# One row of wq ahead of K, and V in one load: reordering the head of a load stream in a decode kernel

## The chip, the cores and the metric

The kernel runs on one core of one Trainium2 chip. The metric is the device time of one execution in microseconds (us), as the median of several runs. The engines are named as in the profile: PE (TensorE) for matrix products, PEld for its weight loads, DVE (VectorE), ACT (ScalarE), POOL (GpSimd) and SP (SyncE), which here does nothing but issue loads and the store of half the result.

## The reference, cut to what matters

One token `x` of 1,024 elements goes through an attention block A and a channel MLP B side by side, both fed by the same layer norm, and both are added to `x`.

```python
xn = layernorm(x)                                     # 1 x 1024
q  = xn @ wq                                          # wq: 1024 x 4096; 32 heads of 128
k, v = k_cache[:, :, -4096:], v_cache[:, :, -4096:]   # 4 key/value heads, the last 4096 of 65536 positions
o  = softmax(q @ k.T * 128**-0.5) @ v                 # 8 query heads to a key/value head
A  = o @ wo                                           # wo: 4096 x 1024
h  = gelu(layernorm(xn) @ w1 + b1)                    # w1: 1024 x 3584
B  = h @ w2 + b2                                      # w2: 3584 x 1024
return x + A + B
```

All inputs are bfloat16. What has to be read from HBM is wq 8 MB, K 4 MB, V 4 MB, w1 7 MB, w2 7 MB and wo 8 MB, nearly 40 million bytes for a single token; every weight is used once.

## The kernel before, in words

Four large SBUF buffers, `slot[0]` to `slot[3]`, each 128 partitions by 32 KB, are used in turn by all the big tensors. K's four heads lie in `slot[0]`, wq's rows 0 to 3 in `slot[1]`, rows 4 to 7 in `slot[2]`; w1's halves follow in `slot[1]` and `slot[0]`, V in `slot[2]`, w2's rows in `slot[3]` and `slot[1]`, wo in `slot[0]` and `slot[2]`. A "row" of wq here is one of the 8 rows of the matrix that a partition holds: `wq_v = A_wq.rearrange("(p c) n -> p c n", p=128)`, so that `wq_v[:, 0, :]` takes 8 KB to each of 128 partitions, 1 MB in all. A load of several neighbouring rows takes one contiguous piece to a partition: 16 KB for two, 32 KB for four.

The program is recorded as a list (`Plan`): each operation names its engine, the keys that it reads and those that it writes. `Plan.emit` turns that into one instruction stream to an engine, in the order of the list, with the semaphore waits that the keys demand. There is no scheduler that reorders. All big loads go through SP's queue in the order of the list; an SP load waits until the readers of its buffer's last contents are done, and what is behind it on SP waits too.

Only the loads of K (`load_k`, four, one to a head, 32 partitions of 32 KB each, L192) and of `x32` (on ACT, L197) stand ahead of the list: they are issued at once, before a barrier that all engines pass at the program's beginning. SP then issues wq in three loads (`wq_cuts`, rows 0 and 1, rows 2 and 3, rows 4 to 7), the two biases, and later w1, V, w2 and wo (all at L211, the helper `dma`).

The steps that the text refers to, in their order:

- POOL makes small constant matrices, PE and DVE make the layer norm (L273 to L311); DVE then turns K in 32 x 32 blocks into `slot[3]` (L332, four transposes, each waits for all four K loads), and DVE (L341) and ACT (L337) copy the blocks into `kT`. w1's second half goes into `slot[0]` when K has been transposed, w2's first rows into `slot[3]` when the copies into `kT` are done.
- PE multiplies wq's rows by the normed token as they come: a loop over rows 0 and 1 (L374), two rows written out, a loop over rows 4 to 7 (L383). The sums are cast into `q_sb`, half on DVE (L386) and half on ACT (L387); eight small products and a cast (L415) make `qm`, and 32 products of `qm` with `kT` give the scores (`sc_ps`).
- The softmax follows: maximum, exponential (ACT, L449) and a DVE transpose of the exponentials into `eTb` (L453). w1's products with the second layer norm (`yT`) lie in between, and gelu makes `hT` and `hTf` (L467, L469).
- PE multiplies `eTb` with V in 32 steps, 30 of them in a loop (L494). All 32 wait for `v_in`, the whole of V.
- 21 rows of w2 are summed by DVE (L478, L481), seven by PE; PE multiplies wo's rows (L225), adds DVE's sum (L549 and a product with ones), and two small casts and two stores end the program.

V is loaded in three parts, which PE waits for together:

```python
for g0, g1 in ((0, 2), (2, 3), (3, 4)):
    dma("sp", v4[:, g0:g1, :, :], A_v_cache[0, g0:g1, Sk - W:Sk, :].rearrange("g (p c) d -> p g c d", p=P), (), (f"v{g0}",), ("slot2",))
v_in = ("eTb", "eTb_pad", "v0", "v2", "v3", "slot2")
```

## Time and profile before

| | before |
|---|---|
| median of 3 runs | 101.05 us (100.94 to 101.19) |
| the profiled execution's own time | 100.79 us |
| its span in the profile | 99.0 us |
| bytes moved | 39.88 MB, mean 403 GB/s over the span |
| busy: PE, DVE, ACT, POOL | 59%, 74%, 31%, 10% |
| granted TensorE clock, mean | 0.862 |

The span runs from the first to the last instruction of the profiled execution; some 1.8 us lie around it. The page gives for each engine the busy share, and for 40 equal slices of the span the busy tenths of each engine, the granted TensorE clock and what the 16 DMA engines moved. The chain that ended last is followed back from the last instruction to what released each one. Views by order of time give the start, the duration, the engine, the line, and in brackets the idle time before it with what ended it. Views by stretches give the busy time of each engine, the granted clock, the DMA share and GB/s. The time of a load "to landing" is from its issue on SP's queue.

### The profile page before, as it was taken

How to read it: one execution, taken by the hardware profiler on the slowest of the kernel's cores; microseconds unless marked ns; L12 is line 12 of the kernel's file. 1: busy time of each engine (PE TensorE's matmuls, PEld its weight loads, DVE VectorE, ACT ScalarE, POOL GpSimd, SP SyncE). 2: the span in 40 equal slices, each digit the busy share in tenths (PEclk: the TensorE clock that was granted, in tenths of full speed). 3: DMA queues.
4: the chain of work that ended last, by engine and by line, in shares of the span. 5: the costliest groups of instructions: out<-in, count | busy, mean ns of one | idle time of the engine just before them, and what ended most of it. 6: DMA issues, size and time to landing. Idle time of an engine off the chain costs nothing.

```text
span 99.0 us, 962 instructions
## 1 busy us (share of the span) xinstructions
PE 58.8 (59%) x323; PEld 16.3 (16%) x220; DVE 73.1 (74%) x75; ACT 30.8 (31%) x29; POOL 9.9 (10%) x22
## 2 busy tenths in 40 slices
PE   0032040497300699957995507987671999994791
PEld 0022000122000233402122102212211111110130
DVE  0024699999999999991045956399989999999231
ACT  0230000899998999920020940000000000000001
POOL 0263560000000580000000000000000000000000
PEclk9999999999965557996699985579998557999999
DMA  1999999999999989988999999999897999999970
GB/s 27 397 424 424 424 424 424 424 450 437 437 450 416 488 371 394 533 371 371 430 427 424 430 434 432 442 424 477 371 544 316 437 424 443 430 437 391 409 300 7
DMA packets 3021, 39.88 MB, mean 403 GB/s; under 512 B 454, under 2 KB 460, under 8 KB 844
## 3 DMA queue, kind: packets, MB, share of 16 engines
q1 hardware_dynamic: 2970, 39.86, 94.9%
q8 instruction: 1, 0.02, 0.1%
q10 hardware_dynamic: 50, 0.00, 0.0%
HBM read 39.86 MB, written 0.00 MB: 403 GB/s over the span
## 4 chain that ended last, share of the span: by engine, by line
DMA 64%; PE 23%; issue 3%; SPq 3%; DVE 0%
DMA slot<-in_A_wq_dram 28%; DMA slot<-in_A_wo_dram 21%; DMA slot<-in_A_v_cache_dram 16%; PE qo_ps L494 12%; PE acc L367 10%; SPq L211 3%; PE acc L231 1%; DVE res L568 0%; PE acc L225 0%
## 5 line engine op out<-in xcount | busy, mean ns | idle before, releaser
L337 ACT COPY kT<-slot 32x1024 bf16<-32x1024 bf16 (+1 forms) x18 | 23.9, 1327 | 12.4 <-DVE slot L332 12.2
L481 DVE SCALAR_TENSOR_TENSOR run<-slot,hTf,run 128x1024 f32<-128x1024 bf16 x20 | 24.2, 1271 | 2.5 <-DMA slot<-in_B_w_dram 2.5
L367 PE MATMUL acc<-slot,xw 128*128 x48 | 15.1, 477 | 13.3 <-DMA slot<-in_A_wq_dram 12.7
L332 DVE STREAM_TRANSPOSE slot<-slot 128x4096 bf16<-128x4096 bf16 x4 | 17.4, 4413 | 0.2 <-DMA slot<-in_A_k_cache_dram 0.2
L494 PE MATMUL qo_ps<-slot,eTb 128*128 (+1 forms) x32 | 11.9, 476 | 6.4 <-DMA slot<-in_A_v_cache_dram 4.2
L341 DVE COPY kT<-slot 32x4096 bf16<-32x4096 bf16 x10 | 13.2, 1319 | 0.2
L225 PE MATMUL sc_ps<-slot,o 128*1 128x512 bf16 x48 | 9.1, 379 | 1.6 <-DMA slot<-in_A_wo_dram 1.6
L367 PEld LDWEIGHTS acc<-slot,xw 128*128 x48 | 5.4, 113 | 23.8 <-issue 21.2
L569 ACT CAST res<-acc 33x224 bf16<-33x224 f32 x1 | 0.3, 339 | 20.4 <-PE acc L225 20.4
L225 PE MATMUL sc_ps<-slot,hT 128*1 128x512 bf16 x14 | 6.1, 626 | 0.4 <-DMA slot<-in_B_w_dram 0.4
L494 PEld LDWEIGHTS qo_ps<-slot,eTb 128*128 (+1 forms) x32 | 3.2, 99 | 15.0 <-issue 12.9
L537 ACT CAST o<-misc 128x32 bf16<-128x32 f32 x1 | 0.2, 185 | 17.4 <-PE misc L231 17.4
L225 PE MATMUL sc_ps<-kT,qm 128*32 128x512 bf16 x32 | 5.3, 853 | 0.3 <-DVE qm L415 0.3
L427 DVE COPY sc<-sc_ps 128x512 f32<-128x512 f32 x1 | 0.7, 692 | 4.9 <-PE sc_ps L225 4.9
L217 PEld LDWEIGHTS <-o 128*1 128x1 bf16 x40 | 2.4, 85 | 11.6 <-issue 11.0
L231 PE MATMUL acc<-spread,qm 32*128 32x512 bf16 x4 | 1.6, 498 | 3.7 <-POOL qm L313 3.7
L231 PE MATMUL misc<-x,spread 32*128 32x8 bf16 x4 | 0.3, 168 | 5.8 <-POOL spread L253 5.8
L247 DVE MEMSET mhalf<- 128x1 f32 x1 | 0.1, 59 | 4.6 <-PEq L201 4.6
L225 PE MATMUL acc<-slot,yT 128*1 128x448 bf16 x64 | 3.4, 353 | 0.0
L426 ACT COPY sc<-sc_ps 128x512 f32<-128x512 f32 x1 | 0.6, 586 | 6.9 <-PE sc_ps L225 6.9
L249 ACT ACT_TABLE_LOAD x1 | 1.3, 1283 | 4.4 <-PEq L201 4.4
L225 PE MATMUL acc<-slot,o 128*1 128x288 bf16 (+1 forms) x32 | 2.2, 272 | 0.7 <-DMA slot<-in_A_wo_dram 0.6
(88 smaller groups left out, 44.2 us busy)
## 6 DMA issues: line engine op xcount, KB each, us to landing
slot<-in_B_w_dram SPq DMA_DIRECT2D x3, 3584.0 KB, 19.1
slot<-in_A_wo_dram SPq DMA_DIRECT2D x3, 2048.0 KB, 26.0
slot<-in_A_k_cache_dram SPq DMA_DIRECT2D x4, 1024.0 KB, 7.9
slot<-in_A_wq_dram SPq DMA_DIRECT2D x2, 2048.0 KB, 16.0
slot<-in_A_wq_dram SPq DMA_DIRECT2D x1, 4096.0 KB, 27.5
slot<-in_A_v_cache_dram SPq DMA_DIRECT2D x1, 2048.0 KB, 11.4
slot<-in_A_v_cache_dram SPq DMA_DIRECT2D x2, 1024.0 KB, 14.5
slot<-in_B_w_dram SPq DMA_DIRECT2D x1, 2048.0 KB, 23.1
```

The source lines that it names most:

```text
L211: plan.add(eng, lambda: q.dma_start(out=out_ap, in_=in_ap), r, w, True, over)
L217: return pe.add_instruction(mybir.InstLdweights(name=nc.get_next_instruction_name(), engine=i.engine, tile_size=(P, 32), tile_position=pos ...
L225: return pe.add_instruction(mybir.InstMatmult(name=nc.get_next_instruction_name(), engine=i.engine, start_tensor_calc=start, stop_tensor_c ...
L231: op("pe", lambda: pe.matmul(out_ap, lhsT=w_ap, rhs=x_ap, start=start, stop=stop, tile_position=pos), r, w)
L249: op("act", lambda: act.activation(out=dummy[:, 0:1], in_=mhalf[0:1, 0:1], func=ACT.Exp), ("mhalf",), ("act_warm",))
L332: op("dve", lambda s=s: dve.transpose(out=scr[:, s, :], in_=k2[:, s, :]), ("k0", "k1", "k2", "k3", "slot0"), (f"scr{s}",))
L337: op("act", lambda s0=s0, s1=s1, R=R, Cd=Cd: act.copy(out=kT[32 * Cd:32 * Cd + 32, R, s0:s1, :].rearrange("p s (c j) -> p (s c) j", j=32), ...
L341: op("dve", lambda R=R, Cd=Cd: dve.tensor_copy(out=kT[32 * Cd:32 * Cd + 32, R, :, :].rearrange("p s (c j) -> p (s c) j", j=32), in_=T3[32 ...
L367: pe.matmul(acc2[:, b, :], lhsT=xw[:, bass.ds(32 * n + 512 * i, P)], rhs=slot[1 + i][:, bass.ds(1024 * n + 512 * b, 512)], start=False, st ...
L427: op("dve", lambda: dve.tensor_copy(out=sc[:, 0:512], in_=sc_ps[:, 0, :]), ("sc0",), ("scs0",))
L481: op("dve", lambda: dve.scalar_tensor_tensor(out=t, in0=wap, scalar=hTf[:, c:c + 1], in1=t, op0=ALU.mult, op1=ALU.add), (key, "hTf", f"run ...
L494: return pe.matmul(qo_ps, lhsT=cols, rhs=v4[:, :, c, :], start=first, stop=last)
```

## The change

wq's row 0 becomes a load of its own, issued on SP as the very first one, ahead of K's four and ahead of the barrier. Row 1 becomes a load of its own, the first behind the barrier; rows 2 and 3, and 4 to 7, are loaded as before. PE's loop over rows 0 and 1 waits for both loads. V goes in one load of four heads instead of three loads. The tensors' places, the arithmetic and the order on the other engines are the same.

```diff
+    wq_v = A_wq.rearrange("(p c) n -> p c n", p=P)
+    wq_sem = nc.alloc_semaphore("wq0")
...
-    for i, sem in [(load_k(g), k_sem[g]) for g in range(Hkv)] + [(nc.scalar.dma_start(out=x32, ...), x_sem)]:
+    for i, sem in [(nc.sync.dma_start(out=slot[1][:, 0:NQ], in_=wq_v[:, 0, :]), wq_sem)] + [(load_k(g), k_sem[g]) for g in range(Hkv)] + [(nc.scalar.dma_start(out=x32, ...), x_sem)]:
...
+    plan.add("sp", lambda: None, (), ("wq0",), wq_sem)
...
-    wq_cuts = ((0, 0, 2), (0, 2, 4), (1, 0, 4))
+    wq_cuts = ((0, 1, 2), (0, 2, 4), (1, 0, 4))
...
-    op("pe", lambda: pe_loop("wq0", 8, wq_rows(0, 1)), ("xw", "wq0"), ("acc2",))
+    op("pe", lambda: pe_loop("wq0", 8, wq_rows(0, 1)), ("xw", "wq0", "wq1"), ("acc2",))
...
-    for g0, g1 in ((0, 2), (2, 3), (3, 4)):
-        dma("sp", v4[:, g0:g1, :, :], A_v_cache[0, g0:g1, Sk - W:Sk, :].rearrange("g (p c) d -> p g c d", p=P), (), (f"v{g0}",), ("slot2",))
+    dma("sp", v_sb.rearrange("p (g n) -> p g n", g=Hkv), A_v_cache[0, :, Sk - W:Sk, :].rearrange("g (p c) d -> p g (c d)", p=P), (), ("v0",), ("slot2",))
...
-    v_in = ("eTb", "eTb_pad", "v0", "v2", "v3", "slot2")
+    v_in = ("eTb", "eTb_pad", "v0", "slot2")
```

More of the change, by code (lines that the diff above doesn't have):

```diff
@@ L196 @@
     x_sem = nc.alloc_semaphore("x32")
-    for i, sem in [(load_k(g), k_sem[g]) for g in range(Hkv)] + [(nc.scalar.dma_start(out=x32, in_=x_flat.rearrange("(a j) -> a j", a=Hq)), x_sem)]:
+    for i, sem in [(nc.sync.dma_start(out=slot[1][:, 0:NQ], in_=wq_v[:, 0, :]), wq_sem)] + [(load_k(g), k_sem[g]) for g in range(Hkv)] + [(nc.scalar.dma_start(out=x32, in_=x_flat.rearrange("(a j) -> a j", a=Hq)), x_sem)]:
         i.then_inc(sem, 16)
@@ L235 @@
     plan.add("act", lambda: None, (), ("x32",), x_sem)
-    wq_v = A_wq.rearrange("(p c) n -> p c n", p=P)
     w1_v = B_w1.rearrange("(p c) n -> p c n", p=P)
@@ L381 @@
                 mm(acc2[32 * t:32 * t + 1, b, :], xw[:, 96 + P * c:97 + P * c], wq_t[0][:, c, j * 512:(j + 1) * 512],
-                   False, False, (0, 32 * t), ("wq0", "wq2", "slot1"), ("acc2",))
+                   False, False, (0, 32 * t), ("wq0", "wq1", "wq2", "slot1"), ("acc2",))
     op("pe", lambda: pe_loop("wq1", 8, wq_rows(1, 2)), ("xw", "wq4", "slot2"), ("acc2",))
```

## The prediction

> **What bounds the kernel now.** I read the page's slices and queues first, then the chain that ended last, then the order of time on each engine.

> ```profile
> span 99.0 us, 962 instructions
> ...
> DMA  1999999999999989988999999999897999999970
> GB/s 27 397 424 424 424 424 424 424 450 437 437 450 416 488 371 394 533 371 371 430 427 424 430 434 432 442 424 477 371 544 316 437 424 443 430 437 391 409 300 7
> ...
> q1 hardware_dynamic: 2970, 39.86, 94.9%
> ...
> DMA 64%; PE 23%; issue 3%; SPq 3%; DVE 0%
> ```

> The DMA row is full from the second slice to the last but two; where a digit falls to 8 or 7, a neighbouring slice moves more than the mean, so these are packet edges and no holes. One queue, SP's, carries all 39.86 MB and keeps 16 engines at work for 94.9% of the span, 94.0 us. The other 5 us are the start, about 2 us before the first data plus the first slices at 27 and 397 GB/s, and the end after the last data. So the kernel is one stream of loads, and its time is start + bytes / rate + tail, as long as the queue never runs empty.

> The chain of waits has its PE parts where a load is long since queued behind:

> ```profile
> 5.28 27.51 DMA slot<-in_A_wq_dram
> ...
> 33.14 9.66 PE acc L367 x32
> ...
> 44.31 15.47 DMA slot<-in_A_v_cache_dram
> ...
> 75.96 20.71 DMA slot<-in_A_wo_dram
> ...
> 96.72 0.30 PE acc L225 x2
> ```

> wq's last row is in at 32.79. V's last load is in at 44.31 + 15.47 = 59.78; between them w1 (two loads of 3,584 KB) and V (4,096 KB), 11.53 MB, passed in 26.99 us, 427 GB/s. Laid end to end at that rate, w1's loads take 8.6 us each and end at 41.4 and 50.0, V (9.8 us) at 59.8, w2's 14 first rows at 68.4, its second 14 at 77.0, half of wo at 86.8. The waits quoted below, which end at 76.90 and 86.70, confirm the last two. The PE stretch from 33.14 lies beside w1's loads and costs nothing.

> **The change, part by part.** In the order of the built program SP now issues wq's row 0, K's four loads, then behind the barrier row 1 (1 MB), rows 2 and 3 (2 MB), rows 4 to 7 (4 MB); later V in one load. Bytes are the same.

> *Rate.* Rows 0 and 1 went as one load with 16 KB to a partition; now they go as 8 KB pieces. V already goes in 8 KB pieces, before and after.

> ```profile
> 50.00:59.00 9.00, 4.70 (x77) 1.39 (x37) 5.97 (x10) 4.19 (x6) 0.00 (x0) 0.99 1.01 425
> ...
> 77.00:91.00 14.00, 13.04 (x46) 2.24 (x24) 13.97 (x13) 0.00 (x0) 0.00 (x0) 0.79 0.99 420
> ...
> 22.00:32.00 10.00, 2.99 (x24) 0.74 (x14) 9.95 (x5) 9.58 (x9) 0.00 (x0) 0.81 0.98 424
> ```

> The last two numbers are DMA share and GB/s. V's 8 KB pieces (first row) make 425 / 1.01 = 421 GB/s for a full share, wo's 16 KB pieces (second) 424, wq's 32 KB pieces (third) 433. 2.10 MB at 421 instead of 424 is 0.04 us, instead of 433 it is 0.14 us. I take +0.05, by the row with the same piece; both ends stay for the range.

> *V in one load.* Two issues on SP and two completions go, one load more for wq comes: one fewer in all.

> ```profile
> slot<-in_A_v_cache_dram SPq DMA_DIRECT2D x1, 2048.0 KB, 11.4
> slot<-in_A_v_cache_dram SPq DMA_DIRECT2D x2, 1024.0 KB, 14.5
> ...
> 43.37 1.40 SPq L211 DMA_DIRECT2D slot<-in_A_v_cache_dram  x3
> ```

> The first V load lands at 43.37 + 11.4 = 54.8 and the third at 59.78: 2 MB and two completions in 5.0 us, which is 421 GB/s, the rate of the whole window. A boundary between queued loads shows no price, so I take 0 for the one fewer; from above, the 0.47 us that one of the three issues takes would be the most it could be worth. The three were waited for together by the same PE instruction, so nothing loses an early part. [...]

> The other side: the first V load held two heads, an HBM distance of 16 MB (65,536 rows of 256 bytes) between a partition's pieces; now four. It took from 50.0 to 54.8, 2.10 MB in 4.8 us = 437 GB/s, no less than the loads of one head. So 0. [...]

> *K behind 1 MB.* At 2.46 us for 1 MB, K is complete 2.5 us later. What hangs on it:

> ```profile
> 13.30 17.42 DVE L332 STREAM_TRANSPOSE slot<-slot 128x4096 bf16<-128x4096 bf16 x4 [0.17 <-DMA slot<-in_A_k_cache_dram]
> ...
> 25.62 5.46 SPq L211 DMA_DIRECT2D slot<-in_B_w_dram  x2
> 30.75 13.31 DVE L341 COPY kT<-slot 32x4096 bf16<-32x4096 bf16 x10
> ...
> 44.10 0.69 DVE L386 CAST q_sb<-acc 128x512 bf16<-128x512 f32 x1
> 44.89 7.77 SPq L211 DMA_DIRECT2D slot<-in_B_w_dram  x3
> 45.49 5.30 PE L225 MATMUL sc_ps<-kT,qm 128*32 128x512 bf16 x32 [0.29 <-DVE qm L415]
> ...
> 55.56 1.25 DVE L453 STREAM_TRANSPOSE eTb<-e 128x1024 bf16<-128x1024 bf16 x1 [0.20 <-ACT e L449]
> 55.70 0.80 SPq L211 DMA_DIRECT2D slot<-in_A_wo_dram  x2
> ...
> 59.98 2.32 PE L494 MATMUL qo_ps<-slot,eTb 128*128 128x512 bf16 x5 [4.17 <-DMA slot<-in_A_v_cache_dram]
> ```

> VectorE starts its transposes only 0.17 us after it is free, so all of it moves: transposes at 15.8 to 33.2, copies to 46.5, q_sb at 46.6, the scores from about 48.0. VectorE is now the late one; wq's products still end at 43.3. Loads that wait behind it on SP: w1's second load goes from 31.1 to 33.6 (queue empty only at 41.4), w2's first from 44.9 to 47.4 (empty at 59.8), the last of the three w2 loads from 52.7 to 55.3 (68.4), wo from 55.7 to 58.4 (77.0). Each stays 7.8 us or more ahead.

> The scores meet another clock:

> ```profile
> 45.00:46.00 1.00, 0.71 (x12) 0.21 (x9) 0.19 (x1) 0.00 (x0) 0.00 (x0) 0.62 0.68 287
> ...
> 48.00:49.00 1.00, 1.00 (x12) 0.17 (x4) 0.00 (x0) 0.00 (x0) 0.00 (x0) 0.67 1.06 459
> 49.00:50.00 1.00, 1.00 (x12) 0.14 (x4) 0.00 (x0) 0.00 (x0) 0.00 (x0) 1.00 0.90 377
> ```

> The granted clock fell in 45 to 46 and came back in 48 to 49, some 3.2 us of the 5.30. With PE idle for 4 us before them, the scores may run slow a little longer: I take 0.2 us, and at most 1.3 us if all of them run at half clock. So eTb, complete at 56.81, comes 2.7 us (at most 3.8) later, at 59.5. V's products start at 59.98 because V lands at 59.78: 3.0 us of cover after some 0.2 us of hand-over. Used up almost, and not exceeded. Past it stand more waits:

> ```profile
> 60.84 0.18 DVE L469 CAST hTf<-hT 128x28 f32<-128x28 bf16 x1
> ...
> 63.54 1.28 DVE L481 SCALAR_TENSOR_TENSOR run<-slot,hTf,run 128x1024 f32<-128x1024 bf16 x1 [2.52 <-DMA slot<-in_B_w_dram]
> ...
> 74.16 2.23 SPq L211 DMA_DIRECT2D slot<-in_A_wo_dram  x5
> 74.17 0.68 DVE L510 TENSOR_TENSOR o_m<-qo_ps,grs 32x512 f32<-32x512 f32 x1 [0.31 <-PE qo_ps L494]
> ...
> 76.90 6.07 PE L225 MATMUL sc_ps<-slot,hT 128*1 128x512 bf16 x14 [0.42 <-DMA slot<-in_B_w_dram]
> ...
> 86.70 3.61 PE L225 MATMUL sc_ps<-slot,o 128*1 128x512 bf16 x16 [0.27 <-DMA slot<-in_A_wo_dram]
> ...
> 91.59 1.89 PE L225 MATMUL sc_ps<-slot,o 128*1 128x512 bf16 x16 [1.28 <-DMA slot<-in_A_wo_dram]
> 93.52 1.28 DVE L549 TENSOR_TENSOR run<-sc_ps,run 33x512 f32<-33x512 f32 x2 [1.78 <-PE sc_ps L225]
> ```

> hTf at 61.02 + 2.7 = 63.7 exceeds VectorE's 2.52 us of waiting for w2 by 0.2 us; the 0.31 at L510 takes that. If V's products slip, PE's waits of 0.42, 0.27 and 1.28 us take 1.97 us before the end moves, and VectorE's 1.78 at L549 as much. wo's last five loads, issued when V's products end at 74.16, are 12 us ahead of their turn. The end is the last wo piece, 96.67. K's delay: 0.

> *wq's products.* Row 1 ends at the same 6 MB of the stream as both rows did, and the loop waits for both; nothing starts earlier.

> *The start.*

> ```profile
> 0.80 2.53 SPq L192 DMA_DIRECT2D slot<-in_A_k_cache_dram  x4
> 4.37 1.35 SPq L211 DMA_DIRECT2D slot<-in_A_wq_dram  x3
> 4.38 0.52 POOL L252 MEMSET spread<- 32x512 bf16 x1 [3.87 <-POOLq L201]
> ...
> 2.00:5.00 3.00, 0.00 (x0) 0.00 (x0) 0.22 (x2) 0.62 (x1) 0.52 (x1) 1.00 0.90 350
> ```

> A fifth issue ahead of the barrier, 2.53 / 4 = 0.63 us, may release all engines at 5.0 instead of 4.37. VectorE was ready at 13.13 and would be at 13.8, with K at 15.8; the next wq issue has 5 MB ahead of it. So 0. What no row shows is how the first load ramps when it is 128 rows of 8 KB instead of 32 rows of 32 KB. In 2 to 5 us, 350 x 3 = 1.05 MB moved where 424 would have moved 1.27 MB: the ramp costs 0.5 us. A better one gains at most that; one twice as slow loses as much. I take 0, since the first load's first byte comes after the same issue at 0.80; ends -0.5 and +0.5.

> **Sum.** 100.79 (the profiled execution: span 99.0 and 1.8 around it) + 0.05 + 0 = 100.84. The median of the runs shown is 101.05, 0.26 above that execution, so 101.1. A measurement of this kernel can tell about 0.3% (0.3 us) from no change.

> **The rivals.**
> - *A faster ramp* (0.23): smaller first pieces spread over more partitions keep all 16 engines busy earlier; the whole stream then ends up to 0.5 us sooner: 100.6. For it: 0.5 us are lost there now. Against: nothing shows that the size of the pieces loses them.
> - *A load costs a fixed sum* (0.02): one load fewer, at most the 0.47 us of an issue by the rows: 100.6. [...] Against: 421 GB/s across two V boundaries.
> - *A slower ramp* (0.22): slower than before. [...] Up to +0.5: 101.6. Against: in the middle of the stream 128-row loads issue in 0.45 us (1.35 / 3), faster than K's.
> - *K's cover is gone* (0.07): the delay of eTb would have to exceed 3.0 + 1.97 = 5.0 us; I find 2.7, at most 3.8. A second delay of the size of K's, 2.5 us, would give 5.2 to 6.3, so +0.2 to +1.3: 101.3 to 102.4.
> [...]

> **How the numbers follow.** My forecast, 101.1 within 100.8 to 101.35, has 0.43: the terms are small and bounded, but the start is unmeasured. Faster: 0.23 + 0.02 = 0.25. Slower: 0.22 + 0.07 + 0.03 = 0.32. The range reaches from the full faster ramp less 0.1 of run spread, 100.5, to the full slower ramp plus 0.15 of spread, 101.8; it leaves out V's pitch, the upper half of the lost cover, and the edges of both ramps, under 2 in 10.

> **What would show it.** Right: transposes of K start at 15.6 to 16.0; q_sb at L386 starts near 46.6 with VectorE, not PE, the late one; V's products start within 0.3 us of 60.0 and still after DMA; PE's wait before 91.59 remains above 0.8 us; the chain ends in wo as before. Wrong: a first slice that moves clearly more or less than 27 + 397 (the ramps); V's products released by eTb and later than 61 (the cover); V's window below 400 GB/s at full share (the pitch); a DMA share with a hole before an issue of SP.

## The result, and the profile after

| | before | change |
|---|---|---|
| first measurement: median | 101.00 us (100.87 to 101.25, 6 runs) | 100.47 us (100.38 to 100.62, 6 runs) |
| ratio to before, 95% interval | | 0.9947 [0.993, 0.9964] |
| two more measurements of the change (100.60, 100.61 us) | | 0.9967 [0.9943, 0.9992], 0.9968 [0.9946, 0.999] |
| profiled execution, span | 100.79 us, 99.0 us | 100.62 us, 98.8 us |

The change makes the kernel faster by 0.3 to 0.5 us. The two profiled executions differ by less, 0.17 us, because the one of before lies 0.2 us under its median and the one of the change 0.15 us above its own; a second profile of the change has a span of 98.6 us.

The page of the change, the DMA rows of its 40 slices and the chain by engine:

```profile
span 98.8 us, 961 instructions
...
DMA  3999979999999999999799999999998999999970
GB/s 50 448 418 451 464 328 458 441 511 438 424 424 405 395 453 453 395 441 464 338 424 424 418 441 413 463 424 429 487 418 383 431 431 424 424 424 405 405 265 1
...
DVE 36%; DMA 32%; PE 20%; issue 5%; SPq 2%; ACT 2%; DVEq 0%
```

Still one stream of loads without a hole. The first two slices moved 50 and 448 GB/s where before they moved 27 and 397: the stream begins sooner. The last slice with loads is emptier (265 against 300): the stream also ends sooner. The chain now names DVE first, since V's products are released by `eTb` in this execution; it still ends in a wo load. The order of time shows the head of the stream and K's path:

```profile
0.80 0.40 SPq L199 DMA_DIRECT2D slot<-in_A_wq_dram  x1
1.26 2.45 SPq L194 DMA_DIRECT2D slot<-in_A_k_cache_dram  x4
4.75 1.29 SPq L213 DMA_DIRECT2D slot<-in_A_wq_dram  x3
...
15.58 17.43 DVE L334 STREAM_TRANSPOSE slot<-slot 128x4096 bf16<-128x4096 bf16 x4 [1.18 <-DMA slot<-in_A_k_cache_dram]
33.00 10.00 PE L369 MATMUL acc<-slot,xw 128*128 x32 [7.58 <-DMA slot<-in_A_wq_dram]
46.36 0.69 DVE L388 CAST q_sb<-acc 128x512 bf16<-128x512 f32 x1
47.77 6.08 PE L227 MATMUL sc_ps<-kT,qm 128*32 128x512 bf16 x32 [0.29 <-DVE qm L416]
58.63 1.25 DVE L454 STREAM_TRANSPOSE eTb<-e 128x1024 bf16<-128x1024 bf16 x1 [0.19 <-ACT e L450]
59.93 0.95 PE L495 MATMUL qo_ps<-slot,eTb 128*128 128x512 bf16 x3 [1.06 <-DVE rs L458]
...
91.47 1.89 PE L227 MATMUL sc_ps<-slot,o 128*1 128x512 bf16 x16 [1.29 <-DMA slot<-in_A_wo_dram]
93.39 1.28 DVE L550 TENSOR_TENSOR run<-sc_ps,run 33x512 f32<-33x512 f32 x2 [1.46 <-PE sc_ps L227]
```

The first load is issued in 0.40 us. K's path is 2.3 us late at its transposes and 3.07 us late at `eTb` (complete at 59.88), and none of that is left at the end: PE waits 1.29 us for wo before 91.47, as it waited 1.28 before. A good clock of the stream is the start of wq's last products, which wait for the first 12.6 MB (K and all of wq): 33.00 here, 33.14 before, 32.79 in the change's second profile. From profile to profile of one kernel this clock scatters by some 0.2 us.

The start itself, in stretches of a quarter of a microsecond (the last two columns are DMA share and GB/s), first the kernel before, then the change:

```profile
1.75:2.00 0.25, 0.00 (x0) 0.00 (x0) 0.00 (x0) 0.00 (x0) 0.00 (x0) 1.00 0.10 8
2.00:2.25 0.25, 0.00 (x0) 0.00 (x0) 0.00 (x0) 0.00 (x0) 0.00 (x0) 1.00 0.92 262
```

```profile
1.75:2.00 0.25, 0.00 (x0) 0.00 (x0) 0.00 (x0) 0.00 (x0) 0.00 (x0) 1.00 1.66 262
2.00:2.25 0.25, 0.00 (x0) 0.00 (x0) 0.00 (x0) 0.00 (x0) 0.00 (x0) 1.00 1.23 197
```

Before, 1.75 to 2.00 us holds nothing but the 2 KB of `x`, and K's first pieces begin in the next stretch. In the change the row's pieces begin a stretch earlier. Shorter stretches narrow it down, again before first:

```profile
1.85:2.10 0.25, 0.00 (x0) 0.00 (x0) 0.00 (x0) 0.00 (x0) 0.00 (x0) 1.00 0.07 6
2.10:2.20 0.10, 0.00 (x0) 0.00 (x0) 0.00 (x0) 0.00 (x0) 0.00 (x0) 1.00 2.29 655
```

```profile
1.75:1.80 0.05, 0.00 (x0) 0.00 (x0) 0.00 (x0) 0.00 (x0) 0.00 (x0) 1.00 0.00 0
1.80:1.85 0.05, 0.00 (x0) 0.00 (x0) 0.00 (x0) 0.00 (x0) 0.00 (x0) 1.00 3.41 492
```

K's first pieces begin between 2.10 and 2.20 us (the 6 GB/s ahead of them are `x`), the row's between 1.80 and 1.85: about 0.3 us sooner.

### The profile page after: what moved, and what is told of

Read it like the earlier page. It is cut to its first block, busy times and chain, and to the rows that moved or that the text cites. A ratio compares the mean times of both kernels' runs of the same rounds, so it can differ in the third digit from the quotient of the medians.

```text
span 98.8 us, 961 instructions
## 1 busy us (share of the span) xinstructions
PE 57.2 (58%) x323; PEld 16.2 (16%) x220; DVE 73.9 (75%) x75; ACT 30.7 (31%) x29; POOL 10.0 (10%) x22
## 2 busy tenths in 40 slices
DMA packets 3132, 39.86 MB, mean 403 GB/s; under 512 B 438, under 2 KB 444, under 8 KB 828
## 3 DMA queue, kind: packets, MB, share of 16 engines
q1 hardware_dynamic: 3082, 39.86, 95.4%
HBM read 39.86 MB, written 0.00 MB: 403 GB/s over the span
## 4 chain that ended last, share of the span: by engine, by line
DVE 36%; DMA 32%; PE 20%; issue 5%; SPq 2%; ACT 2%; DVEq 0%
DMA slot<-in_A_wo_dram 20%; DVE slot L334 18%; DVE kT L343 13%; DMA slot<-in_A_k_cache_dram 13%; PE qo_ps L495 10%; PE sc_ps L227 6%; PE acc L227 2%; SPq L194 2%; ACT e L450 1%; DVE eTb L454 1%; DVE m_loc L435 1%; PE acc L233 1%; DVE q_sb L388 1%; ACT sc L427 1%; DVE res L569 0%
## 5 line engine op out<-in xcount | busy, mean ns | idle before, releaser
L369 PE MATMUL acc<-slot,xw 128*128 x48 | 15.7, 494 | 12.6 <-DMA slot<-in_A_wq_dram 12.2
L495 PE MATMUL qo_ps<-slot,eTb 128*128 (+1 forms) x32 | 10.2, 382 | 5.1 <-issue 4.0
L227 PE MATMUL sc_ps<-kT,qm 128*32 128x512 bf16 x32 | 6.1, 973 | 0.3 <-DVE qm L416 0.3
L227 PE MATMUL sc_ps<-slot,hT 128*1 128x512 bf16 x14 | 4.7, 509 | 0.1
## 6 DMA issues: line engine op xcount, KB each, us to landing
slot<-in_A_wo_dram SPq DMA_DIRECT2D x3, 2048.0 KB, 22.8
slot<-in_A_k_cache_dram SPq DMA_DIRECT2D x4, 1024.0 KB, 9.8
slot<-in_A_wq_dram SPq DMA_DIRECT2D x2, 1024.0 KB, 9.2
slot<-in_A_wq_dram SPq DMA_DIRECT2D x1, 2048.0 KB, 17.8
slot<-in_B_w_dram SPq DMA_DIRECT2D x1, 2048.0 KB, 21.5
```

The lines of the kernel that those rows point to most:

```text
L227: return pe.add_instruction(mybir.InstMatmult(name=nc.get_next_instruction_name(), engine=i.engine, start_tensor_calc=start, stop_tensor_c ...
L369: pe.matmul(acc2[:, b, :], lhsT=xw[:, bass.ds(32 * n + 512 * i, P)], rhs=slot[1 + i][:, bass.ds(1024 * n + 512 * b, 512)], start=False, st ...
L495: return pe.matmul(qo_ps, lhsT=cols, rhs=v4[:, :, c, :], start=first, stop=last)
```

## The experiments

The theory at first: the form of the first load lets the 16 DMA engines start sooner, and that is the whole gain. The rivals: the merged V load, or the smaller pieces of wq.

**The parts of the change, one at a time.** Row first, V in three loads:

```diff
 # the change, but
-    dma("sp", v_sb..., A_v_cache[0, :, ...], (), ("v0",), ("slot2",))
+    for g0, g1 in ((0, 2), (2, 3), (3, 4)): dma("sp", v4[:, g0:g1, :, :], ...)
```

> wq's row 0 ahead of K as in the change, row 1 a load of its own, but V in three loads as before. Start theory (the first load's form lets the 16 DMA engines begin sooner): the whole gain stays, ratio 0.993 to 0.997, DMA in the first 5 us like the change's. V theory (the merged V load is what helps): ratio 0.999 to 1.002. If both give a part, between 0.997 and 0.999.

Only V in one load:

```diff
 # the kernel before, but
-    for g0, g1 in ((0, 2), (2, 3), (3, 4)): dma("sp", v4[:, g0:g1, :, :], ...)
+    dma("sp", v_sb..., A_v_cache[0, :, ...], (), ("v0",), ("slot2",))
```

> The kernel before with V in one load of four heads, nothing else. Start theory: no change, ratio 0.999 to 1.001, DMA in the first 5 us as before. V theory: ratio 0.993 to 0.997. Either way V's window at 50 to 59 us keeps about 425 GB/s; below 400 the HBM pitch would cost.

Only the split of rows 0 and 1, behind K:

```diff
 # the kernel before, but
-    wq_cuts = ((0, 0, 2), (0, 2, 4), (1, 0, 4))
+    wq_cuts = ((0, 0, 1), (0, 1, 2), (0, 2, 4), (1, 0, 4))
```

> The kernel before with wq's rows 0 and 1 as two loads, both behind K and behind the barrier; K first, V in three loads. Start theory: no gain, ratio 1.000 to 1.001 (8 KB pieces instead of 16 KB for 2 MB: +0.04 to +0.14 us). Rival (smaller pieces or one load more help the stream by themselves, wherever they stand): ratio below 0.998.

| | median | ratio to before | span | start of wq's last products |
|---|---|---|---|---|
| row first, V in three | 100.58 us | 0.9972 [0.9957, 0.9987] | 98.7 us | 32.88 |
| V in one | 101.11 us | 1.0025 [1.0001, 1.0049] | 99.0 us | 33.08 |
| rows split | 100.92 us | 1.0009 [0.9992, 1.0027] | 99.0 us | 33.20 |

The row ahead of K carries the gain: its first pieces begin in 1.80 to 1.85 us as in the change. V in one load brings none; if anything it costs (the interval just excludes 1, while the span is that of before). Its stretch 50 to 59 us with four heads in one load:

```profile
50.00:59.00 9.00, 3.19 (x55) 1.01 (x25) 6.68 (x10) 3.68 (x5) 0.00 (x0) 0.91 1.02 431
```

431 GB/s, so the HBM distance of 16 MB between a partition's pieces does nothing here: with V in three loads the same stretch moved 425.

**What makes the start sooner?** First the neighbour in time: `x`, whose 32 pieces go ahead of K's first. Here it is issued behind the barrier:

```diff
 # the kernel before, but
-    ... + [(nc.scalar.dma_start(out=x32, in_=...), x_sem)]
+    dma("act", x32, ..., (), ("x32",))      # in the list, behind the barrier
```

> The kernel before with x's small load on ACT issued behind the barrier instead of beside K's first. Order theory (in the kernel before x's 32 pieces go ahead of K's, in the change behind the row's): K's first data move from about 2.15 us to before 2.0, ratio 0.997 to 0.999. Form theory (K's first load itself takes longer to issue, 0.56 us against 0.40, and starts later): first data stay at 2.1 to 2.2, ratio 0.9995 to 1.001. VectorE's preparation comes up to 3 us later and eats into cover, not into the end.

It measured 100.98 us, 1.0004 [0.9984, 1.0024]; K's first pieces stay where they were:

```profile
1.75:2.00 0.25, 0.00 (x0) 0.00 (x0) 0.00 (x0) 0.00 (x0) 0.00 (x0) 1.00 0.00 0
2.00:2.25 0.25, 0.00 (x0) 0.00 (x0) 0.00 (x0) 0.00 (x0) 0.00 (x0) 1.00 3.99 1049
```

So `x` is not it. Next, a first load of K's own shape, 32 pieces of 32 KB, taken from wq, once to partitions 0 to 31 and once to every fourth partition:

```diff
 # the change, but quarter(i) = slice(32*i, 32*i+32), then slice(i, P-3+i, 4)
-    nc.sync.dma_start(out=slot[1][:, 0:NQ], in_=wq_v[:, 0, :])
+    nc.sync.dma_start(out=slot[1][quarter(0), :]..., in_=wq_v[quarter(0), 0:4, :])
...
+    for i in (1, 2, 3): dma("sp", wq_t[0][quarter(i), :, :], wq_v[quarter(i), 0:4, :], (), (f"wq{i}",))
```

> The change, but its first load is wq's rows 0 to 3 of partitions 0 to 31 (32 pieces of 32 KB, 1 MB, neighbouring partitions), the other three quarters behind the barrier. Row-number theory (128 pieces of 8 KB spread over 128 partitions start sooner than 32 of 32 KB): it starts like K, first data at 2.1 to 2.2, ratio 0.999 to 1.002. Stride theory (K's partitions 4 apart cost 0.16 us of issue): issue 0.40 us, first data before 2.0, ratio 0.994 to 0.998.

> As the run with the quarter of neighbouring partitions, but the quarter is every fourth partition, K's own pattern. Stride theory: issue 0.55 us or more, first data at 2.1 to 2.2, ratio 0.999 to 1.002, unlike its neighbour. Row-number theory: both alike, at K's start. Order of tensors (wq instead of K first, whatever the form): both alike and like the change, 0.994 to 0.998.

The first issue and the first stretches, neighbouring partitions, then every fourth:

```profile
0.80 0.40 SPq L202 DMA_DIRECT2D slot<-in_A_wq_dram  x1
...
1.75:2.00 0.25, 0.00 (x0) 0.00 (x0) 0.00 (x0) 0.00 (x0) 0.00 (x0) 1.00 6.23 1442
...
17.50:32.00 14.50, 0.00 (x0) 0.00 (x0) 13.85 (x4) 9.28 (x9) 0.00 (x0) 1.00 0.96 208
```

```profile
0.80 0.56 SPq L202 DMA_DIRECT2D slot<-in_A_wq_dram  x1
...
1.75:2.00 0.25, 0.00 (x0) 0.00 (x0) 0.00 (x0) 0.00 (x0) 0.00 (x0) 1.00 0.08 7
2.00:2.25 0.25, 0.00 (x0) 0.00 (x0) 0.00 (x0) 0.00 (x0) 0.00 (x0) 1.00 3.70 919
```

The same tensor, the same number and size of pieces, other partitions. Neighbouring ones: issued in 0.40 us, data before 2.00. Every fourth: 0.56 us, data after 2.00, like K. The pieces' distance in HBM differs too (64 KB and 256 KB), but K's pieces lie side by side in HBM and start late all the same. This settles the start on the step between partitions, and rules out the number of rows. In the shorter stretches all five profiles with every fourth partition first (the kernel before, V in one, rows split, `x` late, the strided quarter) begin between 2.10 and 2.20 us (0 to 8 GB/s before 2.00). The change's three profiles, the row with V in three, two rows, four rows, half a row and the block of 32 begin between 1.80 and 1.85 (131 to 1442 GB/s from 1.75 to 2.00). (A piece is counted where it begins, so shares above 1 are only beginnings.)

The times, 111.40 us (1.1044 [1.0993, 1.1094]) and 101.37 us (1.0038 [1.0011, 1.0064]), say less on the start. The block of 32 partitions loses 10 us for another reason: its other three quarters run from 17.5 to 32 us at 208 GB/s, half the rate, while the strided quarters keep theirs (421 GB/s from 14 to 20 us). Why the neighbouring ones get half of it no run shows. K on every fourth partition pays with a slow start, but does not pay this: 419 GB/s from 5 to 12.5 us in the kernel before.

The strided quarter is 0.2 us above the range expected of it, and the start is not the reason. Its last products of wq begin at 33.15 us, as before (33.14): wq ahead of K gains nothing in this form. What it loses comes later. PE waits for all four quarters before it begins, so their buffer comes free late, and w1's first load is issued at 30.92 instead of 25.62, some 2 us before the queue runs empty. The stretch from 31 to 36 us, first before, then here:

```profile
31.00:36.00 5.00, 2.86 (x7) 1.09 (x8) 4.96 (x4) 4.98 (x3) 2.78 (x3) 0.50 0.97 415
```

```profile
30.92 2.62 SPq L216 DMA_DIRECT2D slot<-in_B_w_dram  x2
...
31.00:36.00 5.00, 2.54 (x11) 1.05 (x11) 4.94 (x4) 4.64 (x4) 2.71 (x2) 1.00 0.99 378
```

415 / 0.97 = 428 GB/s for a full share before, 378 / 0.99 = 382 here: over 5 us about 0.5 us of stream. That the late issue is the cause is likely, but no run moved it alone.

**How large, and in what pieces?** Two rows, four rows, half a row, an eighth of a row, and two half rows first, each with what remains of wq behind the barrier:

```diff
 # the change, but the first load is
-    out=slot[1][:, 0:NQ], in_=wq_v[:, 0, :]             # 8 KB pieces, 1 MB
+    rows 0 and 1: wq_v[:, 0:2, :]                       # 16 KB pieces, 2 MB
+    rows 0 to 3: wq_v[:, 0:4, :]                        # 32 KB pieces, 4 MB
+    half a row: wq_v[:, 0, 0:2048]                      # 4 KB pieces, 0.5 MB
+    an eighth: wq_v[:, 0, 0:512]                        # 1 KB pieces, 128 KB
+    two half rows: wq_v[:, 0:2, 0:2048]                 # 4 KB pieces, 1 MB
```

> wq's rows 0 and 1 as one first load (2 MB, 128 rows of 16 KB pieces) ahead of K; V in one load; K so 4.9 us later than in the kernel before. Start theory by the number of rows (128 against K's 32): the first data come as early as in the change (DMA in 2 to 5 us as there); by the size of the piece (8 KB against 32 KB): about half of the gain at the start. Cover theory: eTb comes 2.4 us later than in the change, at 62.3; VectorE's last sum, which waits 1.46 us there, is then 1.0 us late and the end moves by about 0.9 us: 101.2 to 101.6 us, ratio 1.002 to 1.006. If the cover holds: 100.4 to 100.6.

> The kernel with rows 0 and 1 as one first load once more, to see whether it is better than the change (ratio 0.9967 in its second measurement): the start theory gives it the same start and 16 KB pieces instead of 8 KB for 2 MB, worth 0.04 to 0.14 us: ratio 0.994 to 0.998, not to be told from the change.

> Rows 0 and 1 as one first load, on the same chip as the change: if the 16 KB pieces are worth something it is 0.04 to 0.14 us of rate plus a smaller spread of the 16 engines at the start: 0.1 to 0.2 us under the change (ratio to before 0.993 to 0.996); if not, equal within 0.1 us.

> wq's rows 0 to 3 as one first load (4 MB, 32 KB to a partition) ahead of K; V in one load; K about 9.5 us later than in the kernel before. The start is the change's. Cover theory: eTb at about 65.0, V's products released by it, VectorE's rows of w2 end at about 97 instead of 92, the end moves by 3 to 4.5 us: 103.5 to 105 us, ratio 1.026 to 1.041. If K's place costs nothing at all: 100.4 to 100.7, ratio 0.995 to 0.998.

> The change with a first load of half a row (4 KB to each of 128 partitions, 0.5 MB); the rest of rows 0 and 1 in one load behind the barrier. Bridge theory (a first load with neighbouring partitions starts data at 1.83 us, and its bytes keep the engines busy until K's slower first load has data, at about 1.26 + 1.35 = 2.6 us): 0.5 MB last 1.2 us, to 3.0, so the gain stays: ratio 0.994 to 0.998. Size theory (the gain needs the whole row, or 8 KB pieces): ratio 0.999 to 1.001.

> The same with an eighth of a row first (1 KB to a partition, 128 KB, 0.3 us of data). Bridge theory: data start at 1.83 us, end at about 2.2, and nothing more comes before K's at about 2.6: K is issued 0.46 us later than in the kernel before and only 0.3 us of bytes are ahead of it, so no gain or a small loss: ratio 0.999 to 1.003. Rival (waking the engines early is what counts, whatever the size): ratio 0.994 to 0.998.

> The change with a first load of the first halves of rows 0 and 1: 1 MB as in the change, but in 4 KB pieces; the second halves in one load behind the barrier, in 4 KB pieces too (1 MB more of them: +0.1 us). Bytes theory (the half row was too few bytes to bridge K's slow start): the gain is back, ratio 0.995 to 0.999, and wq's rows 4 to 7 are in by 32.8 to 33.1 us. Pieces theory (4 KB pieces ramp badly, whatever their number): ratio 1.000 to 1.004, rows 4 to 7 in at 33.3 us or later, as with the half row (33.42).

The change ran beside them twice more:

> The changed kernel itself once more, beside the others on one chip: ratio 0.993 to 0.998; first data before 2.0 us, the first load in the queue issued in 0.40 us.

> The changed kernel once more, for its spread from profile to profile and for the comparison with the next run: ratio 0.994 to 0.998, wq's rows 4 to 7 in at 32.7 to 33.0 us.

| first load | pieces | median | ratio to before | start of wq's last products |
|---|---|---|---|---|
| one row (the change, second and third) | 8 KB | 100.60, 100.61 us | 0.9967, 0.9968 | 32.79 |
| two rows | 16 KB | 100.46, 100.48, 100.60 us | 0.9978 [0.9949, 1.0008], 0.9953 [0.9936, 0.9969], 0.9968 [0.9944, 0.9992] | 32.71, 32.81, 32.67 |
| half a row | 4 KB | 101.03 us | 1.0004 [0.9989, 1.0018] | 33.42 |
| two half rows | 4 KB | 101.62 us | 1.0057 [1.0034, 1.008] | 33.85 |
| an eighth | 1 KB | 101.75 us | 1.0089 [1.0062, 1.0115] | 33.74 |
| four rows | 32 KB | 105.52 us | 1.0367 [1.0317, 1.0416] | 32.84 |

The stream's clock, in the order second change, two rows (third), half a row, two half rows:

```profile
32.79 9.36 PE L369 MATMUL acc<-slot,xw 128*128 x32 [7.29 <-DMA slot<-in_A_wq_dram]
```

```profile
32.67 3.56 PE L369 MATMUL acc<-slot,xw 128*128 x8 [8.19 <-DMA slot<-in_A_wq_dram]
```

```profile
1.75:2.00 0.25, 0.00 (x0) 0.00 (x0) 0.00 (x0) 0.00 (x0) 0.00 (x0) 1.00 1.15 131
...
33.42 9.28 PE L370 MATMUL acc<-slot,xw 128*128 x32 [7.54 <-DMA slot<-in_A_wq_dram]
```

```profile
1.75:2.00 0.25, 0.00 (x0) 0.00 (x0) 0.00 (x0) 0.00 (x0) 0.00 (x0) 1.00 0.64 98
...
33.85 2.74 PE L370 MATMUL acc<-slot,xw 128*128 x6 [7.60 <-DMA slot<-in_A_wq_dram]
```

The half row begins before 2.00 us too, and loses it again: the bridge theory, by which 0.5 MB were enough, is refuted. With 1 MB in 4 KB pieces it is worse still (1.0057, beyond the 1.004 expected of it), so it is the pieces and not the bytes. The eighth loses more than either theory gave it (1.0089). Pieces of 8, 16 and 32 KB all gain.

Not all of that loss lies at the start, because what is left of rows 0 and 1 behind the barrier is cut otherwise too: 12 KB pieces behind the half row, 4 KB pieces behind the two half rows. These pass between 14 and 20 us, in the second change, the half row and the two half rows:

```profile
14.00:20.00 6.00, 1.83 (x5) 0.62 (x6) 5.03 (x4) 0.15 (x1) 0.37 (x1) 1.00 0.94 399
14.00:20.00 6.00, 1.15 (x3) 0.41 (x4) 5.75 (x4) 0.88 (x1) 0.37 (x1) 1.00 1.03 427
14.00:20.00 6.00, 0.74 (x3) 0.21 (x2) 3.89 (x1) 0.00 (x0) 0.61 (x1) 1.00 0.97 388
```

For a full share these are 424, 415 and 400 GB/s; against the change 0.13 and 0.34 us over the 6 us. The rest of the lag of 0.63 and 1.06 us, about 0.5 and 0.7, is there before. At the start every piece takes longer than its bytes. The rows of 1.75 to 2.00 us tell by how much: the share times 0.25 us times 16 engines, divided by the number of pieces that the GB/s make, is 0.58 and 0.43 us for a 4 KB piece (half row, two half rows) and 0.83 for an 8 KB piece (the change's first profile), where 424 GB/s over 16 engines would give 0.15 and 0.31. So an opening piece of 4 KB pays 0.3 to 0.4 us above its bytes and one of 8 KB 0.5, for twice the data. What that time is no run shows. Two rows and one row can't be told apart, and no version beats the change clearly.

Four rows first put K's transposes at 22.64 instead of 13.30. The start is as early as the change's, and the cover (the time by which K's path may slip before the end moves) is gone:

```profile
66.55 0.96 PE L495 MATMUL qo_ps<-slot,eTb 128*128 128x512 bf16 x3 [1.06 <-DVE rs L458]
...
97.33 1.23 DVE L518 TENSOR_TENSOR run<-run 128x1024 f32<-128x1024 f32 x1
...
99.40 1.24 PE L233 MATMUL acc<-run,ones_f 128*1 128x288 f32 x6 [1.83 <-DVE run L550]
```

V's products start at 66.55, VectorE's sum of w2 ends at 98.6 instead of 91.8, and PE waits for VectorE at the end. The time is 0.5 us beyond the 103.5 to 105 expected: the scores took 6.62 us, and `eTb` came at 66.49, not 65.0. With two rows first K is 4.5 us late (transposes at 17.78) and nothing moves at the end. My expectation for that run, 0.9 us from a cover gone, was a miss: I moved `eTb` by the whole delay, but the copies ran 12.3 us instead of 13.3 (from 35.2 to 47.5; in the change from 33.0 to 46.3), the scores 5.08 us instead of 6.08, and `eTb` came out at 60.10, 0.2 us behind the change's. Between 4.5 and 9.3 us of delay at the transposes the end gives way. A span of 103.8 against 98.7 would put the edge at 9.3 - 5.1 = 4.2 us if the end moved one for one; the 4.5 us of two rows, which cost nothing, say that it lies somewhat higher. No run measured the edge itself.

## Why the prediction was right or wrong

**The start: the step that failed.** I put the ramp at 0, "since the first load's first byte comes after the same issue at 0.80". It doesn't. Both issues begin at 0.80, but K's first takes 0.56 us and its data begin at 2.10 to 2.20; the row's takes 0.40 and its data begin at 1.80 to 1.85. The term was about -0.3 us and not 0: the stream's clock stands at 33.14, 33.08, 33.20 and 33.15 with K or the strided quarter first (before, V in one, rows split, strided quarter), and at 33.00, 32.79 and 32.88 with the row first (two profiles of the change, the row with V in three); the medians say -0.3 to -0.5. It stood inside my bounds of -0.5 and +0.5, and the rows for it were quoted: issues of 0.63 us for K and 0.45 for wq. I used them against a slower ramp, and did not see that with nothing queued ahead the issue stands in front of the first byte. The issues differ by 0.16 us, about half of the 0.3; why the data of every fourth partition also come later after their issue (0.74 to 0.84 us, against 0.60 to 0.65) stays open.

Of the 0.6 us between 101.1 and the first 100.47, the start is 0.3; 0.05 is the median of before (101.00 for 101.05) and 0.05 my term for the rate, which no run resolves. The other 0.2 is not repeated by the two later measurements. The sign that I named for a ramp came: 50 and 448 GB/s in the first two slices instead of 27 and 397, some 0.18 MB or 0.4 us of stream.

**The faster ramp**, which I gave 0.23, is what happened, at a time of 100.6 that two measurements gave (100.60, 100.61) and the first undercut (100.47, 0.03 below my range). That the number fits is partly luck, since its reason was wrong: not smaller pieces on more partitions, but neighbouring partitions; smaller pieces lose (101.03 and 101.62 us with 4 KB pieces against 100.60 with 8 KB).

**K's delay costs nothing: right**, by the waits that I named, though one sign failed. In the change's first profile V's products are released by `eTb`, not by V, since the scores took 6.08 us where I had allowed 5.5; in its second they took 5.44 and V's products waited 1.50 us for V again, at 59.54. The end keeps to the stream in both: in the second both wq's last products and the last cast are 0.2 us sooner. The cover that I put at 5.0 us of delay of `eTb` is smaller by one estimate: with four rows `eTb` was 9.7 us late (66.49 against 56.81) and the span 5.1 us longer than the change's, which leaves 4.6 if the end moved one for one.

**V in one load is worth nothing: right**, with no sign of a fixed sum to a load nor of the HBM pitch (431 GB/s). The 0.03 among the chances of slower was for V at half rate; no run shows that, V's window moved 431 GB/s with V in one load alone and 423 in the change (49.5 to 58.5 us). **The smaller pieces for 2 MB at +0.05: not resolved**, 1.0009 with 1 inside its interval. **The barrier** let SP go on at 4.75, not 5.0, and the stream had most of 5 MB queued by then.

**The chances.** With 0.43 on no change I trusted that a stream without holes can't be shortened; here it could at its start, by about 0.3 us.

## What to carry to other kernels

Where one queue of loads bounds a kernel, look at what comes before its first byte: the first load should be one that is quick to issue and ramps well, with slower forms queued behind it. Here that was a load in pieces of 8 KB or more on neighbouring partitions over all 128: issued in 0.40 us, where K's form took 0.56, and some 0.3 us sooner with its first data. Before moving a load back in such a queue, add up the waits on its consumer's path; here 4.5 us were free and 9.3 were not.
